# The second phase of an attention and gated-MLP kernel: seven block products for eight of its feed-forward blocks instead of four

## The chip, the cores and the metric

The kernel runs on one core of a Trainium2 chip, as one program. The metric is the device time of that program in microseconds (us). The engines named below are TensorE (PE; its weight loads are PEld), VectorE (DVE), ScalarE (ACT) and SyncE (SP, whose queue issues all the DMAs). SBUF is the memory on the core, PSUM holds what TensorE accumulates, in banks of 512 fp32 columns.

## The reference

```python
def phi(x):
    proj = np.einsum('bhsd,df->bhsf', x, w_phi)
    proj = proj - np.max(np.abs(proj), axis=-1, keepdims=True)
    return np.concatenate([np.exp(proj), np.exp(-proj)], axis=-1)
q_p, k_p = phi(q), phi(k)                       # 8 batches, 8 heads, 576 tokens, 64 -> 256
kv = np.einsum('bhsf,bhsd->bhfd', k_p, v)
num = np.einsum('bhsf,bhfd->bhsd', q_p, kv)
den = np.einsum('bhsf,bhf->bhs', q_p, np.sum(k_p, axis=2))[..., None] + 1e-06
x = (num / den).transpose(0, 2, 1, 3).reshape(4608, 512)
gate = 1.0 / (1.0 + np.exp(-(x @ w_gate)))      # 512 -> 1536
return (gate * (x @ w_val)) @ w_out             # 1536 -> 512
```

## The kernel before

The 4608 tokens of `x` go through the feed-forward part in twelve blocks `j` of 128 of its 1536 features. To keep near fp32 accuracy, each operand of a matmul is split into a high part of type fp32r and the remainder, and each product is three matmuls (high x high, high x low, low x high).

First phase: attention over 32 pairs of heads (`attend`), and, as soon as 512 tokens of `x` (a chunk, nine in all) are there, the blocks 0 to 3 on that chunk (`first_js`). `gate` computes one block's gate and value products, 12 matmuls of 512 columns each (L909), and `mm_out` the output product (L957). The partial sums of the four blocks go to DRAM (`yscr`), the chunks of `x` too (`xscr`). The gate is made of Tanh(g/2) and Exp(g) on ScalarE, and on VectorE of a mask (L933) and two multiplies with the value (L938, L943); the factor 2 that this leaves is taken out by the 0.5 in the output's scale (L980, L1109).

Second phase: blocks 4 to 7 in the same way on all nine chunks (`gate(NCH + C, j, ...)`), with the chunks of `x` fetched and split again (`load_x`, L884 to L893), the partial sums of the first phase added (`finish`, L1109) and written to DRAM again (`y2scr`). Then blocks 8 to 11 with seven block products instead of eight: the 768 x 512 block of `x` is cut into four quarters, from which `x_blocks` makes seven operands (fetches L1180, subtractions L1191, splits L1200 on ScalarE and L1204 on VectorE), `combine` makes seven operands of the weights of a pair of blocks (L1043, L1057, L1066, L1071), `group` does the seven products of 6 matmuls of 384 columns (L1247) and adds their results up on VectorE (L1260), `gated` and `valued` make `h` (L1285 to L1327), and the output product is L1354. A pass over 768 tokens has four groups (two pairs of blocks, gate and value) and 72 output matmuls; six such passes (`dc`) cover the tokens. The weights of each matrix come packed as 64-bit words and are unpacked by `weigh` (load L788, then L793 to L864 on VectorE, L797 and L826 on ScalarE).

Memory: `Area.ring` cuts four arenas into slots; slots of different stages overlap, and a slot is taken when its last user has ended. `low` and `flat` are there from the start, `high` and `more` take the place of the attention's tiles when these are done (`swap`).

Order: the code only lists operations with a rank, their inputs, outputs and slots. `Plan.run` puts them into one list per engine by a planner: of the operations that could start soonest, the one of lowest rank. Each engine runs its list in order, so an operation that waits holds all that stands behind it, DMA issues on SP's queue included.

Of the kernel before, what the change touches and what calls it, by code (L numbers as in the profile page):

```python
# [20 lines left out]
P = 128  # L21
NP = H // 2
DM = H * D
# [11 lines left out]
JB = 8  # L35
# [5 lines left out]
RB = 84 << 10  # L41
FB = 3 << 10
NQ4 = JB - JA
NQ = 3
ONPE = 12
# [13 lines left out]
HSTEP = 2.0  # L59

# [206 lines left out]
def attention_moe(  # L267
# [62 lines left out]
    wscr = [dram.tile([2, P, DM], F32, tag=f"wo{c}", name=f"wo{c}") for c in range(NJ - JB)]  # L330
# [7 lines left out]
    r_wh, r_wl = (x.ring(JA, 3 * DM) for _ in range(2))  # L338
    r_xh, r_xl = (x.ring(XN, CW) for _ in range(2))
    r_hh, r_hl = (x.ring(HN, CW) for _ in range(2))  # L340
# [4 lines left out]
    r_top = x.ring(2, DM, U32)  # L345
    x = high()
    r_w2 = x.ring(2 * NQ4, 3 * DM)
    r_wh2, r_wl2 = r_w2[::2], r_w2[1::2]
    r_zh, r_zl = x.ring(6, CW), x.ring(6, CW)
    r_k = x.ring(6, CW)  # L350
    x = low(56)
    r_zh2, r_zl2 = r_zh + x.ring(2, CW), r_zl + x.ring(2, CW)
    r_y1 = x.ring(4, DM)
    r_wst = x.ring(7, DM)
    r_G = low().ring(8, 7 * 2 * P)
    r_X = low(56).ring(10, 2 * HT)
    x = high()
    r_X += x.ring(4, 2 * HT)
    r_h = x.ring(8, 2 * HT)
    r_y1b = x.ring(4, DM)  # L360
    r_wo = high(48).ring(8, DM)
    r_f = flat().ring(5, HT)
    x = flat(12)
    r_tmp = x.ring(3, 2 * HT)
    r_f += x.ring(7, HT) + more().ring(FB // (4 * HT), HT)
# [18 lines left out]
    def on_act(n, fn, reads, writes, rank):  # L384
        return plan.op("ACT", 0.08 + n / 1200, 0.17, fn, reads, writes, rank)
# [17 lines left out]
    closing, opening, feeding = [], [], []  # L403
# [467 lines left out]
    def weigh_all(j, r, step, deep, rings):  # L871

        wh, wl = Buf([rings[0]], [P, 3 * DM]), Buf([rings[1]], [P, 3 * DM])
        weights[j] = [(wh, wl), []]
        for m in range(3):
            weigh(j, m, r + step * m, deep(m), wh, wl, slice(m * DM, m * DM + DM), m)
# [22 lines left out]
    def gate(c, j, r, banks, parted=False, rings=(r_hh, r_hl)):  # L899
# [3 lines left out]
        def product(o, m, c0, c1):  # L903
            (wh, wl), _ = weights[j]
# [20 lines left out]
        u, t = Buf([r_u], [P, CW]), Buf([r_t], [P, CW])  # L925
        hh, hl = Buf([rings[0]], [P, CW]), Buf([rings[1]], [P, CW])
        z = -100.0
        on_act(CW, lambda: act.activation(t(), g(), AF.Tanh, scale=0.5), [g], [t], z)  # L928
        on_act(CW, lambda: act.activation(u(), g(), AF.Exp), [g], [u], z)  # L929

        def positive():
# [14 lines left out]
        on_act(CW, lambda: act.copy(hh(), u()), [u], [hh], z)  # L946
        dve(
            CW, lambda: vec.tensor_tensor(hl(), u(), hh().bitcast(F32), op=ALU.subtract),  # L948
            [u, hh], [hl], z,
        )  # L950
        return hh, hl

    def mm_out(acc, t, hs, j, first, last):
        (hh, hl), (wh, wl) = hs, weights[j][0]
        ts, ws = slice(t * P, t * P + P), slice(2 * DM, 3 * DM)
        for i, (a, w) in enumerate(((hh, wh), (hh, wl), (hl, wh))):
            nc.tensor.matmul(  # L957
                acc(), a()[:, ts], w()[:, ws], start=first and i == 0, stop=last and i == 2
            )

    def first_js(c, r, step):
# [5 lines left out]
        for t in range(CW // P):  # L967
            acc, y = Buf(banks, [P, DM]), Buf([r_y], [P, DM])

            def go(t=t, acc=acc):  # L970
# [5 lines left out]
                [x for h in hs for x in h] + [(x, 2) for i in range(JA) for x in weights[i][0]],  # L976
# [3 lines left out]
                DM, lambda y=y, acc=acc: act.activation(y(), acc(), AF.Copy, scale=0.5),  # L980
# [7 lines left out]
    for i in range(N):  # L988
# [4 lines left out]
        if i < 4:  # L993
            weigh_all(
                i, WAT + 3 * WSTEP * i, WSTEP, lambda m, i=i: 3 * i + m >= RAW, (r_wh, r_wl)
            )
        if i % NP == NP - 1:
            lo = 0 if i < NP else ((i // NP) * S) // CW
            for c in range(lo, ((i // NP + 1) * S) // CW):
                r = due(i + 1) + LEAD + 66.0 * (c - lo)  # L1000
                if c:
                    fed = len(plan.ops)
                    load_x(c, r - 20.0, [(r_xh, r_xl)])
                    feeding += plan.ops[fed:]
# [15 lines left out]
    for j in range(JA, JB):  # L1020
        weigh_all(j, base + 10.0 * (j - JA), 3, lambda m: False, (r_wh2, r_wl2))

    blocks, wo, combined = {}, {}, []
    names = ["11", "12", "S3", "22", "S1", "S2", "S4"]
    KH = 2 * P

    def combine(n, m, r):

        gh, gl = Buf([r_G], [P, 7 * KH]), Buf([r_G], [P, 7 * KH])
        blocks[n, m] = gh, gl  # L1030
        w, x = Buf([r_mid], [P, 4 * KH], F32), Buf([r_mid], [P, 4 * KH], F32)

# [3 lines left out]
        for i in range(2):  # L1036
            weigh(
                JB + 2 * n + i, m, r + 3 * i, False, gh, gl,
                slice(2 * i * KH, 2 * (i + 1) * KH), i, [done],
# [7 lines left out]
                [(gh, i), (gl, i)], [(w, i)], r + 5, after=combined[-1:],  # L1047
            )
        for o, a, b, op, reads in (
            (0, (w, 2), (w, 3), ALU.add, [(w, 1)]),  # L1050
            (1, (x, 0), (w, 0), ALU.subtract, [(w, 0)]),
            (2, (w, 1), (x, 1), ALU.subtract, [(w, 0)]),
            (3, (w, 0), (w, 2), ALU.subtract, [w]),
# [4 lines left out]
                    of(x, o), of(*a), of(*b), op=op  # L1058
                ),
                reads, [x], r + 5.5 + o / 10,  # L1060
            )
        combined.append(plan.ops[-1])
        for n_, o, i in ((3, 4, 0), (1, 2, 3)):
            part = 2 if o == 4 else 1
            on_act(
                n_ * KH, lambda n_=n_, o=o, i=i: act.copy(of(gh, o, n_), of(x, i, n_)),  # L1066
# [365 lines left out]
```

## Time and profile before

| | |
|---|---|
| median of 3 runs (lowest to highest) | 1185.74 us (1184.75 to 1186.16) |
| the profiled execution | 1183.81 us |
| its span, first to last instruction | 1182.0 us |
| TensorE's clock | 1.0 throughout |
| end of attention's matmuls | 514 us |
| first matmul of the first seven-product pass | 901 us |
| last matmul | 1178.4 us |

The page gives the busy time of each engine over the span, the waits tell whom an engine waited for, the chain is the work that ended last followed back from the end, and windows give busy times for a stretch. In a timeline the first number is the start, the second the length of an instruction from start to end; instructions of one engine overlap a little at their ends, so that the distance between two starts is what an instruction costs in a row of them. Matmuls are pipelined: their lengths (337 to 395 ns) say nothing, the distance between their starts does.

### The profile page before, as it was taken

Reading aid. Unit: us, or ns where it says so; the run is one execution under the profiler, and the core shown is the slowest. Engines: PE = TensorE matmul, PEld = TensorE weight load, DVE = VectorE, ACT = ScalarE, POOL = GpSimd, SP = SyncE. Lnnn points to the kernel's source line nnn. Section 1 sums busy time; section 2 is a strip of 40 time slices with the busy share of each in tenths; the row PEclk is TensorE's granted clock in tenths of the full one; section 3 lists DMA queues with packets and bytes.
Section 4 is the critical chain, followed back from the end, with each engine's and each line's share of the span. In section 5 each row is a group of like instructions: output and inputs, shape, how many; then the busy total and the mean of one; then the engine's idle time right before and its main releaser. Section 6 shows DMA issues by size and latency. Waiting matters only on the chain.

```text
span 1182.0 us, 21892 instructions
## 1 busy us (share of the span) xinstructions
PE 1166.2 (99%) x8652; PEld 928.0 (79%) x8652; DVE 904.0 (76%) x1755; ACT 591.4 (50%) x1128; POOL 0.7 (0%) x6
## 2 busy tenths in 40 slices
PE   8999999999999999999999999999999999999998
PEld 6676666667766767778888888888888999999997
DVE  6999989888888788669836997444446978878885
ACT  6867776666666566545533453232223443433432
POOL 0000000000000000000000000000000000000000
PEclk9999999999999999999999999999999999999999
DMA  6764553533444342334416544223333235135132
GB/s 232 217 223 139 159 186 89 171 116 113 133 134 137 86 157 87 113 108 157 141 36 226 173 145 169 95 84 107 120 123 110 60 105 157 42 120 161 41 108 72
DMA packets 90223, 152.18 MB, mean 129 GB/s; under 512 B 18312, under 2 KB 33800, under 8 KB 90120
## 3 DMA queue, kind: packets, MB, share of 16 engines
q1 hardware_dynamic: 90120, 150.78, 40.3%
q8 instruction: 68, 1.11, 0.4%
q14 instruction: 35, 0.29, 0.1%
HBM read 110.62 MB, written 39.98 MB: 127 GB/s over the span
## 4 chain that ended last, share of the span: by engine, by line
PE 83%; DVE 8%; DMA 5%; ACT 2%; issue 1%; SPq 0%; DVEq 0%
PE gate L909 22%; PE bank L1247 14%; PE bank L957 9%; PE gate L1354 8%; PE bank L909 7%; PE gate L957 6%; PE bank L618 4%; PE bank L660 3%; DMA rb<-den 2%; PE bank L429 2%; PE bank L678 2%; DMA den<-dn 1%; PE bank L534 1%; DVE d L584 1%; PE bank L632 1%
## 5 line engine op out<-in xcount | busy, mean ns | idle before, releaser
L909 PE MATMUL gate<-low 128*128 128x512 f32 x744 | 177.0, 394 | 1.2 <-ACT flat L929 0.6
L909 PEld LDWEIGHTS gate<-low 128*128 128x128 f32 x744 | 137.7, 188 | 31.6 <-issue 1.2
L1247 PE MATMUL bank<-low 128*128 128x384 f32 x728 | 151.9, 337 | 0.4 <-DVE low L1204 0.4
L1247 PEld LDWEIGHTS bank<-low 128*128 128x128 f32 x728 | 129.0, 188 | 1.2 <-DVE low L1204 0.7
L909 PE MATMUL gate<-high 128*128 128x512 f32 x468 | 113.6, 390 | 0.0
L476 ACT ACTIVATE ek<-ek 128x512 f32<-128x512 f32 (+1 forms) x192 | 96.7, 526 | 27.9 <-DVE ek L464 26.6
L957 PE MATMUL bank<-high 128*128 128x512 f32 x432 | 105.1, 392 | 0.2 <-DVE high L948 0.2
L909 PEld LDWEIGHTS gate<-high 128*128 128x128 f32 x468 | 87.9, 188 | 18.7
L1354 PE MATMUL gate<-high 128*128 128x512 f32 x432 | 99.1, 390 | 0.0
L957 PEld LDWEIGHTS bank<-high 128*128 128x128 f32 x432 | 81.0, 188 | 18.2 <-DVE high L948 0.6
L1354 PEld LDWEIGHTS gate<-high 128*128 128x128 f32 x432 | 81.1, 188 | 16.5
L957 PE MATMUL gate<-low 128*128 128x512 f32 x384 | 92.8, 395 | 0.0
L938 DVE SCALAR_TENSOR_TENSOR flat<-flat,gate 128x512 f32<-128x512 f32 x66 | 45.2, 685 | 57.8 <-PE gate L909 57.2
L957 PEld LDWEIGHTS gate<-low 128*128 128x128 f32 x384 | 70.9, 188 | 15.4 <-issue 1.0
L618 PE MATMUL bank<-ek,vin 128*32 128x256 f32 x1240 | 73.3, 381 | 4.0 <-ACT d L542 3.2
L933 DVE TENSOR_SCALAR flat<-flat 128x512 uint32<-128x512 uint32 x72 | 30.2, 419 | 58.9 <-ACT flat L928 58.9
L618 PEld LDWEIGHTS bank<-ek,vin 128*32 128x32 f32 x1240 | 37.5, 110 | 45.1 <-issue 9.8
L1247 PE MATMUL bank<-high,low 128*128 128x384 f32 x280 | 72.3, 335 | 0.0
L1260 DVE TENSOR_TENSOR flat<-flat,bank 128x384 f32<-128x384 f32 x98 | 54.0, 551 | 20.2 <-PE bank L1247 19.5
L946 ACT CAST high<-flat 128x512 fp32r<-128x512 f32 x36 | 22.3, 621 | 90.6 <-DVE flat L943 90.6
L435 DVE TENSOR_REDUCE mk<-bank 128x4 f32<-128x512 f32 (+1 forms) x92 | 49.1, 553 | 19.8 <-PE bank L429 17.1
L943 DVE SCALAR_TENSOR_TENSOR flat<-flat 128x512 f32<-128x512 f32 x72 | 49.6, 689 | 4.0
(210 smaller groups left out, 2049.2 us busy)
## 6 DMA issues: line engine op xcount, KB each, us to landing
flat<-w_moe SPq DMA_DIRECT2D x36, 512.0 KB
low<-xs SPq DMA_DIRECT2D x49, 256.0 KB
kin<-k SPq DMA_DIRECT2D x32, 320.0 KB
qin<-q SPq DMA_DIRECT2D x32, 320.0 KB
vin<-v SPq DMA_DIRECT2D x32, 320.0 KB
ys<-flat SPq DMA_DIRECT2D x36, 256.0 KB
yt<-flat SPq DMA_DIRECT2D x36, 256.0 KB
high<-yt SPq DMA_DIRECT2D x36, 256.0 KB
```

Of the source, the lines that this page charges most:

```text
L435: vec.tensor_reduce(mx, pk, axis=AX.X, op=ALU.max, apply_absolute_value=True)
L476: lambda g=g, sg=sg: act.activation(ek[g]()[:, :, sg * F : sg * F + F], ek[g]()[:, :, F:], AF.Exp, scale=1.0 - 2.0 * sg,),
L618: nc.tensor.matmul(o_[o : o + Q, : 2 * F], vx()[:, 2 * t + hd, o % D : o % D + Q], (e0, e1)[hd][:, t, :] if t < 4 else e2[:, 0, :], start= ...
L660: nc.tensor.matmul(nm()[o : o + Q, :], w()[:, sg, o : o + Q], es[sg]()[:, o // D, cs], start=sg == 0, stop=sg == 1, tile_position=(0, o),)
L909: nc.tensor.matmul(o(), a()[:, ws], x(), start=cc + n == 0, stop=cc == NC4 - 1 and n == 2,)
L933: vec.tensor_scalar(tu, tu, 0x7FFFFFFF, None, op0=ALU.bitwise_and)
L938: lambda: vec.scalar_tensor_tensor(t(), t(), 1.0, vl(), op0=ALU.add, op1=ALU.mult),
L943: lambda: vec.scalar_tensor_tensor(u(), u(), 1.0, t(), op0=ALU.min, op1=ALU.mult),
L957: nc.tensor.matmul(acc(), a()[:, ts], w()[:, ws], start=first and i == 0, stop=last and i == 2)
L1247: nc.tensor.matmul(o()[:, :HT], s()[:, ws], y()[:, cc, :], start=first and cc + i_ == 0, stop=cc + i_ == 3, skip_group_check=not first,)
L1260: lambda: vec.tensor_tensor(o(), p(), q()[:, :HT], op=ALU.add),
L1354: nc.tensor.matmul(acc(), s()[:, h, o : o + P], w(), start=n + i + k_ == 0, stop=n == NB - 1 and i == 1 and k_ == 2,)
```

## The change

- Blocks 4 to 7 of the second phase are done like blocks 8 to 11. There are two passes of six times 768 tokens: one over the pairs of blocks (4,5) and (6,7), with the partial sums of the first phase going to `y2scr`, one over (8,9) and (10,11), which ends in `out`. The same slots serve both.
- The combined weights of the first pass are made at the end of the first phase, straight into the slots `r_G` and `r_wo` of the `high` arena. Those of the second pass are made during the first four 768-token steps of the first pass, one matrix pair and one output matrix a step, in two staging slots (`r_stage`), written to DRAM (`kept`, to `gscr` and `wscr`) and fetched into the first pass's slots as these come free (`fetched`). The blocks of `x` (`r_X`) now lie in `low` where the first phase's weights lie.
- From chunk 7 of the first phase on, the gate is ScalarE's Sigmoid and one multiply, with no factor 2; `exps` keeps these behind every earlier operation of ScalarE.

```diff
+    if c >= LATE:                                   # in gate(); LATE = 7
+        on_act(CW, lambda: act.activation(u(), g(), AF.Sigmoid), [g], [u], z, exps)
+        dve(CW, lambda: vec.tensor_tensor(u(), u(), vl(), op=ALU.mult), [vl], [u], z)
+    else:
+        halved(g, vl, u, z)
...
-    for C in range(NCH):
-        r0 = base + 200.0 + span * C
-        load_x(NCH + C, r0 - 20.0, [(r_zh2, r_zl2) if C > 1 else (r_zh, r_zl)], [last] + [fed] * (C > 1))
-        for i, j in enumerate(js):
-            hs = gate(NCH + C, j, r, [r_g, r_a], False, (r_k, r_k))
-            for t in range(4):
-                pe(
-                    "f", 0.685,
-                    lambda acc=acc, t=t, hs=hs, j=j, i=i: mm_out(
-                        acc, t, hs, j, i == 0, i == len(js) - 1
-                    ),
...
-    for dc in range(NDC):
-        r = base2 + 46.0 * dc
-        x = x_blocks(dc, r - 20.0)
+    def pass_over(ns, dc, r, ws, wo, src, mark, dst, dmark):
+        x = x_blocks(dc, r - XLEAD)
+        for i, n in enumerate(ns):
+            hs.append([(Buf([r_h], [P, 2, HT]), Buf([r_h], [P, 2, HT])) for _ in range(2)])
+            gs = gated(group(ws[n, 0], x, r + 14.6 * i))
+            valued(gs, group(ws[n, 1], x, r + 14.6 * i + 7.3), hs[i])
...
+    for n in range(2):
+        r = base - 30.0 + 30.0 * n
+        for m in range(2):
+            ws[n, m] = combine(n, m, r + 10.0 * m, [r_G], [])
+        for j in pair(n):
+            wo[j] = out_weight(j, r + 20.0, [r_wo], [])
+    start = base + 150.0
+    for dc in range(NDC):
+        r = start + SPAN * dc
+        pass_over((0, 1), dc, r, ws, wo, yscr, ymark, lambda c, t: y2scr[c][t], y2mark)
+        if dc < 4:
+            n, m = 2 + dc // 2, dc % 2
+            kept(combine(n, m, r + KEEP, [r_stage], [done]), gscr[n, m], mark, r + KEEP)
+            j = JA + 4 + dc
+            kept(out_weight(j, r + KEEP + 10.0, [r_stage], [done]), wscr[j], mark, r + KEEP)
+    start += SPAN * NDC
+    for n, m, late in ((2, 0, []), (2, 1, taken[-4:-3]), (3, 0, outs[-8:-7]), (3, 1, outs[-1:])):
+        ws[n, m] = fetched([r_G], 7 * KH, gscr[n, m], marks[n, m], start, late)
+    for j in (*pair(2), *pair(3)):
+        wo[j] = fetched([r_wo], DM, wscr[j], marks[j], start + 10.0)
+    for dc in range(NDC):
+        pass_over((2, 3), dc, start + SPAN * dc, ws, wo, y2scr, y2mark, final, None)
```

The changed kernel's lines stand elsewhere: L913 and L970 are the full gate and output products, L1228 and L1310 those of the seven-product form, L1241 its adds, L1279 and L1287 the multiply and the remainder of `h`, L1177 and L1190 the subtractions and splits of `x`, L795 to L866 the unpacking of weights, L1068 to L1093 their combination, L1138 the sum with the partial result, L1166 the fetches of `x`, L1133 those of partial sums, L1142 the results' stores, L1106 and L1117 the weights' way to DRAM and back.

How the order moves, at three places. First TensorE's list at the end of the first phase (`gate` and `bank` are PSUM banks, `low` and `high` the arenas of the operands). Before:

```order
L909 MATMUL bank4_192<-low_313 128x512 x12
L909 MATMUL gate1_201<-low_313 128x512 x12
L957 MATMUL bank0_168<-high_5431 128x512 x3
L957 MATMUL bank3_182<-high_5431 128x512 x3
L957 MATMUL bank2_180<-high_5431 128x512 x3
L957 MATMUL bank1_170<-high_5431 128x512 x3
L909 MATMUL gate0_194<-high_5431 128x512 x12
L957 MATMUL gate2_207<-low_313 128x512 x12
```

Now:

```order
L913 MATMUL bank3_194<-low_325 128x512 x12
L1228 MATMUL bank2_192<-low_325,high_5441 128x384 x6
L1228 MATMUL bank1_182<-low_325,high_5441 128x384 x6
L970 MATMUL gate1_213<-low_325 128x512 x12
L970 MATMUL gate0_206<-low_325 128x512 x12
L970 MATMUL gate2_219<-low_325 128x512 x12
L970 MATMUL bank0_180<-low_325 128x512 x12
L1228 MATMUL bank4_204<-low_325,high_5441 128x384 x6
```

The second phase's full products (operands in `high`), which were woven into the end of the first phase, are gone; two products of the first seven-product group come ahead of the last chunk's output products.

Second, VectorE's list in the last group of a seven-product step (`flat` and `more` hold sums on the way). Before, in the first step:

```order
L1296 TENSOR_SCALAR flat_163<-flat_163 128x384 x2
L1260 TENSOR_TENSOR flat_163<-flat_163,bank4_192 128x384
L1260 TENSOR_TENSOR more_7935<-flat_163,bank0_168 128x384
L1260 TENSOR_TENSOR more_7935<-more_7935,bank2_180 128x384
L1191 TENSOR_TENSOR flat_163<-flat_163,low_313 128x768
L1309 SCALAR_TENSOR_TENSOR more_7935<-more_7935,bank3_182 128x384
```

Now, in the second step of the first pass:

```order
L1241 TENSOR_TENSOR flat_175<-flat_175,bank0_180 128x384
L850 SCALAR_TENSOR_TENSOR flat_175<-flat_175 128x512
L1241 TENSOR_TENSOR more_5903<-flat_175,bank3_194 128x384
L858 TENSOR_SCALAR flat_175<-flat_175 128x512
L795 TENSOR_SCALAR flat_175<-flat_175 128x512
L1241 TENSOR_TENSOR more_5903<-more_5903,bank1_182 128x384
L1177 TENSOR_TENSOR flat_175<-more_5903,low_325 128x768
L1279 TENSOR_TENSOR flat_175<-flat_175,bank4_204 128x384
```

Steps of the weights' unpacking stand between the adds; the masks (L1296) are gone.

Third, SP's list in the last step of the first pass; before, each such step had only the quarters of `x`, partial sums and results there:

```order
L1166 DMA more_5903<-xs1_89 128x2x256
L1117 DMA high_5441<-g20_127 128x1792 x2
L1166 DMA low_325<-xs0_88 128x2x384
L1166 DMA low_325<-xs0_88 128x2x128
L1117 DMA high_5441<-g21_128 128x1792 x2
L1166 DMA low_325<-xs0_88 128x2x384
L1166 DMA low_325<-xs1_89 128x2x256
L1117 DMA high_5441<-g30_129 128x1792 x2
L1133 DMA low_325<-ys8_105 128x512
L1142 DMA yt7_113<-flat_175 128x512
```

The second pass's combined weights (`g20` to `g30`) are fetched between the quarters of its first block of `x`.

More of the change, by code (lines that the diff above doesn't have):

```diff
@@ L345, in attention_moe @@
     r_top = x.ring(2, DM, U32)
-    x = high()
[L347 to L361, printed above, removed]
+    x = low()
+    r_X = x.ring(14, 2 * HT)
+    r_y1 = x.ring(3, DM)
+    r_h = x.ring(8, 2 * HT)
+    r_stage = x.ring(2, 7 * 2 * P)
+    x = high()
+    r_G = x.ring(8, 7 * 2 * P)
+    r_wo = x.ring(8, DM)
+    r_x7 = high(42).ring(2 * NC4, CW)
+    r_sum = flat(20).ring(1, 2 * DM)
+    r_tmp = flat(24).ring(1, 2 * HT)
     r_f = flat().ring(5, HT)
-    x = flat(12)
-    r_tmp = x.ring(3, 2 * HT)
-    r_f += x.ring(7, HT) + more().ring(FB // (4 * HT), HT)
+    x = more()
+    r_tmp += x.ring(2, 2 * HT)
+    r_f += x.ring(6, HT)
     at_rings = {}
@@ L903, in product @@
         def product(o, m, c0, c1):
-            (wh, wl), _ = weights[j]
+            wh, wl = weights[j][0]
             for cc in range(c0, c1):
@@ L999, in attention_moe @@
             for c in range(lo, ((i // NP + 1) * S) // CW):
+                if c == LATE:
+                    exps.append(
+                        plan.op(
+                            "X", 0.0, 0.0, lambda: None,
+                            after=[o for o in plan.ops if o.eng == "ACT"],
+                        )
+                    )
                 r = due(i + 1) + LEAD + 66.0 * (c - lo)
@@ L1046, in combine @@
                 ),
-                [(gh, i), (gl, i)], [(w, i)], r + 5, after=combined[-1:],
+                [(gh, i), (gl, i)], [(w, i)], r + 5,
             )
[L1049 to L1053, printed above, removed]
+        for o, a, b, op in (
+            (3, 2, 3, ALU.add),
+            (2, 0, 2, ALU.subtract),
+            (0, 3, 0, ALU.subtract),
+            (1, 1, 0, ALU.subtract),
         ):
@@ L1108, in finish @@
             DM,
-            lambda: vec.scalar_tensor_tensor(
-                y(), acc(), 0.5, y1().bitcast(F32), op0=ALU.mult, op1=ALU.add
-            ),
+            lambda: vec.tensor_tensor(y(), acc(), y1().bitcast(F32), op=ALU.add),
             [acc, y1], [y], -90.0,
         )
-        sp(256 << 10, lambda: nc.sync.dma_start(dst(c, t), y()), [y], mark(c, t), r)
-        return got
-    js = list(range(JA, JB))
-    span = 33.0
-    y2mark = [Buf() for _ in range(NCH)]
-    loads = []
@@ L1148, in attention_moe @@
-    turn = plan.op("X", 0.0, 0.0, lambda: None, after=loads + staged)
-    base2 = base + 200.0 + span * NCH
-    for j in range(JB, NJ):
-        wo[j] = Buf([r_wo], [P, DM]), Buf([r_wo], [P, DM])
-        for n in range(2):
-            sp(
-                256 << 10,
-                lambda x=wo[j][n], j=j, n=n: nc.sync.dma_start(
-                    x().bitcast(F32), wscr[j - JB][n]
-                ),
-                [wmark[j, n]], [wo[j][n]], base2 - 10.0, [turn],
-            )
+        sp(
+            256 << 10, lambda: nc.sync.dma_start(dst(c, t), y()), [y],
+            [(dmark[c], t)] if dmark else [], r,
+        )
@@ L1227, in x_blocks, with group @@
         return at_
-    prior = [turn]
-    XB = ("11", "T2", "T3", "T1", "21", "T4", "22")
-    taken = [turn]
-    def group(n, m, x, r):
-        gh, gl = blocks[n, m]
+    def group(weight, x, r):
+        gh, gl = weight
         a, b, c, d = (Buf([r_a], [P, CW]) for _ in range(4))
```

272 lines of the change are left out of this document (127 added, 145 removed).

## The prediction

> **What bounds the kernel now.** I read the head of the page first, then the chain that ended last in order of time, TensorE's list of waits, busy time by stage, and last VectorE's instructions one by one. The page and the waits (us in total, times, longest):
>
> ```profile
> span 1182.0 us, 21892 instructions
> PE 1166.2 (99%) x8652; PEld 928.0 (79%) x8652; DVE 904.0 (76%) x1755; ACT 591.4 (50%) x1128; POOL 0.7 (0%) x6
> HBM read 110.62 MB, written 39.98 MB: 127 GB/s over the span
> PE bank L429 <- DMA kin<-k: 4.4, 1, 4.4
> PE bank L1247 <- DVE low L1204: 0.4, 1, 0.4
> PE bank L957 <- DVE high L948: 0.2, 1, 0.2
> ```
>
> TensorE is busy all the time, and in the second phase it waits for 0.4 and 0.2 us only. So the kernel is as long as its list of matmuls, and the question has two parts: how much shorter the list gets, and whether the others keep up with the new one. The chain gives start, length and count of each stretch:
>
> ```profile
> 514.41 16.54 PE gate L909 x72
> 703.74 5.44 PE gate L909 x24
> 736.38 5.52 PE gate L909 x24
> 933.92 16.33 PE gate L1354 x72
> 995.94 29.32 PE bank L1247 x168
> 1162.01 16.38 PE gate L1354 x72
> 1178.41 0.69 DVE flat L1109
> ```
>
> A 512-column matmul takes 5.44/24 = 0.2267 us, in every second chunk 5.52/24 = 0.2300; a 384-column one of the seven-product form takes 29.32/168 = 0.1745. The stages, and a stretch in which the DMA engines are loaded (busy us of PE, PEld, DVE, ACT and POOL with counts; then PE clock, DMA share, GB/s):
>
> ```profile
> 522.90:613.20 90.30, 68.68 (x127) 1.00 0.40 129
> 530.00:540.00 10.00, 10.00 (x46) 8.24 (x45) 9.19 (x19) 7.64 (x15) 0.00 (x0) 1.00 0.56 211
> 640.00:650.00 10.00, 10.00 (x45) 8.26 (x44) 9.81 (x20) 2.39 (x6) 0.00 (x0) 1.00 0.87 290
> 950.26:979.55 29.29, 29.29 (x169) 29.29 (x169) 21.49 (x46) 12.68 (x26) 0.00 (x0) 1.00 0.33 98
> 995.94:1041.59 45.65, 45.65 (x241) 42.84 (x241) 38.30 (x71) 18.50 (x35) 0.00 (x0) 1.00 0.34 103
> ```
>
> (The first of these rows is VectorE alone.) A seven-product pass over 768 tokens takes TensorE 45.65 us. VectorE is busy for 38.30 of them, the highest of the others, and idle for 7.35: it is the engine to watch.
>
> **TensorE's list.** Until 514.41 both lists are the same. From there to 933.92, 419.5 us, TensorE does what is left of the first phase, 34 units of 12 matmuls (ten of chunk 6, twelve each of chunks 7 and 8), 34 x 12 x 0.2267 = 92.5 us; the groups of one seven-product pass, 29.3; and the full products of blocks 4 to 7. These are left: 419.5 - 92.5 - 29.3 = 297.7 us for 108 units, 1296 matmuls, the two waits among it. The change takes them out and puts in six more passes of 168 + 72 matmuls, 6 x (29.32 + 16.33) = 273.9. **Net -23.8 us.** The profiled execution took 1183.81, its span 1182.0; with -23.8 and nothing else it would be 1160.0.
>
> The gain per column is thinner than 7/8, since a shorter matmul pays the same fixed part: 384 columns cost 0.1745/0.2267 = 77% of 512, not 75%. And PEld is busy for 29.29 of 29.29 us while the groups run. The Trainium skill (Perfetto Trace Analysis, Identifying the Most-Contended Engine) asks to judge TensorE's headroom by LDWEIGHTS busy time instead of matmul busy time; by that rule the groups are at the limit of the weight loads and shorter matmuls bring nothing more. The trace does not contradict it, but the 0.1745 was measured under these very loads, so the sum stands either way.
>
> Bounds. The products now read weights from the high arena and blocks from low; before, 728 of 1008 read low alone and the rest both, at one pace, so 0. The output products of all twelve passes take `h` from low and weights from high. L1354 has both in high (16.33 for 72). The other end is the chunk whose operands lie in both: 864 x (0.2300 - 0.2267) = 2.9 us. I take **+1.0**, nearer to L1354.
>
> **The handover.** VectorE's paces, from instructions that followed each other without a wait (start, us):
>
> ```profile
> 558.79 0.42 DVE L856 TENSOR_SCALAR flat<-flat 128x512 uint32<-128x512 uint32 x1
> 559.12 0.42 DVE L793 TENSOR_SCALAR flat<-flat 128x512 uint32<-128x512 uint32 x1
> 559.46 0.69 DVE L864 SCALAR_TENSOR_TENSOR high<-flat 128x512 fp32r<-128x512 uint32 x1
> 560.06 0.68 DVE L938 SCALAR_TENSOR_TENSOR flat<-flat,bank 128x512 f32<-128x512 f32 x1
> 546.00 0.69 DVE L820 SCALAR_TENSOR_TENSOR flat<-flat 128x512 uint32<-128x512 uint32 x1
> 546.72 0.43 DVE L840 TENSOR_SCALAR flat<-flat 128x512 uint32<-128x512 uint32 x1
> 963.79 0.55 DVE L1316 SCALAR_TENSOR_TENSOR flat<-flat 128x384 f32<-128x384 f32 x1
> 964.26 0.55 DVE L1260 TENSOR_TENSOR flat<-flat,bank 128x384 f32<-128x384 f32 x1
> 989.10 0.94 DVE L1204 TENSOR_TENSOR low<-flat,high 128x768 fp32r<-128x768 f32 x1
> 989.97 1.81 DVE L1204 TENSOR_TENSOR low<-flat,low 128x768 fp32r<-128x768 f32 x2
> L1057 DVE TENSOR_TENSOR flat<-flat 128x256 f32<-128x256 f32 x16 | 6.7, 421 | 0.0
> 522.90 0.69 DVE L864 SCALAR_TENSOR_TENSOR high<-flat 128x512 fp32r<-128x512 uint32 x1
> ```
>
> So 0.34 us for a mask of 512, 0.60 for a two-operand step of 512, 0.47 of 384, 0.87 of 768, and 0.42 less the overlap of 0.08 = 0.34 of 256; a step that reads its predecessor's result starts 0.72 after it instead of 0.60, some 0.13 more. Before, the first write to the new arena was at 522.90. In the new list VectorE has 146 instructions from there to the last part of the first blocks: 70 x 0.60 + 64 x 0.34 + 11 x 0.87 + 0.47 = 73.8 us. The last part is wanted by the seventh product, at 514.4 + 92.5 + 6 x 1.05 = 613.2, so 90.3 us are there and 16.5 are left for waits. The same stretch held 68.68 us of VectorE before without harm. One place is late by my count: chunk 8's last value product ends at 596.1, VectorE then owes two steps of 0.60 and T2's remainder of 0.87, and the second early product wants it at 597.1. **+1.3** for the handover. Ends: 0, and 8 if half of the 16.5 us turns out to be missing.
>
> ScalarE gains a table load in this stretch, because Sigmoid follows Exp and Tanh. The row of the one at the start:
>
> ```profile
> L476 ACT ACT_TABLE_LOAD x1 | 1.3, 1283 | 0.7 <-PEq L1382 0.7
> ```
>
> 1.3 us once, on an engine that is 50% busy and loses an Exp or a Tanh from each gate: 0. The Trainium skill (ScalarE: Activation LUTs, What ACT_TABLE_LOAD costs) adds a drain of 1.38 us to each switch; no run here shows it. By it the handover would be 2.7 us on ScalarE and, at worst, as much later.
>
> **The passes.** Each pass loses eight masks and eight multiplies on VectorE. What stays is 36 steps of 384, 11 of 768 and 6 of 512: 16.9 + 9.6 + 3.6 = 30.1 us of 45.65. The first four carry a weight preparation each: three matrices of 3 x 0.34 + 3 x 0.60 = 2.8, two sums of 512 and eight steps of 256, in all 8.5 + 1.2 + 2.7 = 12.4, so 42.5 us. That leaves 3.1 us of each 45.65, where 7.35 were idle. I laid the paces along the order of the second pass, from the start G of its last group to the next pass's start at G + 7.3 + 16.3 = G + 23.7: the five adds and the weight steps between them follow the banks; the eight value steps end at G + 11.4; the last block part ends at G + 21.6, and the product that wants it comes at G + 30; the next pass's first add is due at G + 26.0, and VectorE is free for it at G + 25.9. No product waits, but hardly any slack is left. **+1.0** for the four; 0 to 26, the rival below. The eight unloaded passes: 0.
>
> **The turn between the passes.** 8 x 0.92 MB of block weights and 8 x 0.26 MB of output weights are read back, 9.4 MB, while some 6.3 MB of x, partial sums and results also move, between the first free slot, 7 us into the last pass, and the first output products, 29 us into the next: 67.5 us. At the 290 GB/s above that is 54 us, at 211 it is 74. The block loads stand ahead of loads and stores on SP's queue, which then wait too, but for work due later. **+1.0**, from 0 to 7.
>
> Sum: 1160.0 + 1.0 + 1.3 + 1.0 + 1.0 = 1164.3. The median of the runs, 1185.74, lies 1.9 above the profiled execution; so **1166 us**.
>
> **Rivals.**
> *VectorE bounds the loaded passes (ends slower).* If the 7.35 us of idle time stay, because they are waits for transfers and for ScalarE that the order doesn't fill, and each of the 18 steps of the weight chains runs as a dependent one (+0.13, 2.3 us), a loaded pass takes 42.5 + 7.35 + 2.3 = 52.2, +6.5, and four cost 26: 1162.9 + 26 = 1189. It decides from 6 us a pass, 23.8/4. For it: 93% load. Against it: the weight steps stand between the adds, where VectorE now waits for TensorE. 5%. In between, with 2 to 5 us a pass, it is 1171 to 1183, about 1176: 15%.
> *The turn.* At 211 GB/s 7 us late: 1172. 7%.
> *The saving isn't there.* If weight loads, with their 188 ns each,
>
> ```profile
> L1247 PEld LDWEIGHTS bank<-low 128*128 128x128 f32 x728 | 129.0, 188 | 1.2 <-DVE low L1204 0.7
> ```
>
> set the pace of the new passes, each takes 168 x 0.188 + 16.33 = 47.9 and the list shrinks by 10.2 only: 1179. 29.32 for 168 speaks against it. 4%.
> *Little moves*, by several of these: 1%.
>
> **How the numbers follow.** The forecast has 68%. The range goes from 1160 (no stall, and no difference between profiled execution and median) to 1178, which takes in the turn and most of the half-bound passes. A measurement tells about 0.2% (2.4 us) from no change. Faster: 68 + 15 + 7 + 4 less the 1 of the in-between case that ends too near = 93%; same 1 + 1 = 2%; slower 5%.
>
> **What would show it.** Right: 2016 seven-product matmuls at 0.1745, twelve passes of some 45.7 us, VectorE over 41 us busy in the first four and near 32 later, TensorE's waits under 5 us beyond those at the start. Wrong: passes one to four longer than the rest, with waits of L1228 for VectorE or ScalarE; a gap at the first pass or at the turn; an unequal pace of L1228 or L1310.

## The result, and the profile after

The changed kernel takes 1167.3 us (median of 4 runs, 1165.75 to 1167.91), the kernel before 1185.95 beside it (4 runs, 1184.75 to 1186.37): a ratio of 0.9842, 95% interval 0.9825 to 0.9859. The profiled execution took 1167.91 us with a span of 1166.0. The forecast was 1166 with a range from 1160 to 1178.

The head of the page after, and TensorE's waits from 500 us to the end (us in total, times, longest):

```profile
span 1166.0 us, 22301 instructions
PE 1148.7 (99%) x8796; PEld 939.5 (81%) x8796; DVE 933.6 (80%) x1793; ACT 583.3 (50%) x1115; POOL 0.7 (0%) x6
HBM read 117.96 MB, written 47.32 MB: 142 GB/s over the span
```

```profile
PE bank L1228 <- DVE low L1190: 0.7, 1, 0.7
PE bank L1228 <- ACT low L1186: 0.2, 1, 0.2
```

The number of matmuls rises from 8652 to 8796, TensorE's busy time falls by 17.5 us: many matmuls of 512 columns have become more of 384. VectorE and the traffic grow, and TensorE waits for little: 0.9 us from 500 us to the end, at the first two seven-product groups. The chain, in order of time:

```profile
516.39 16.54 PE gate L913 x72
...
557.83 8.40 PE gate L913 x36
...
613.37 27.04 PE bank L1228 x156
640.41 16.79 PE gate L1310 x72
657.21 29.13 PE bank L1228 x168
...
870.01 13.99 PE gate L1310 x60
...
890.97 24.97 PE bank L1228 x144
```

Three things are to be seen. The steps follow each other without a gap: five steps of 29.13 + 16.79 after 640.41 end at 870.01, which is where the sixth's output products start, and the turn to the second pass (870 to 916) has no hole either. The output products are slower than L1354 before, 16.79 for 72 instead of 16.33; the product groups are a little faster, 29.13 for 168 instead of 29.24 to 29.32 in the five full stretches before. And the first row, up to which both kernels have the same list, starts 1.98 us later than its counterpart at 514.41.

VectorE's busy time in the six steps of the first pass:

```profile
613.40:659.20 45.80, 39.05 (x72) 1.00 0.46 148
659.20:705.10 45.90, 43.41 (x80) 1.00 0.60 193
705.10:751.00 45.90, 43.48 (x83) 1.00 0.62 205
751.00:797.00 46.00, 43.75 (x82) 1.00 0.54 176
797.00:843.00 46.00, 35.26 (x63) 1.00 0.47 151
843.00:889.00 46.00, 32.05 (x54) 1.00 0.55 192
```

Up to 43.75 of 46.00 us, and in this execution still nobody waits. The preparation does not keep to steps 1 to 4: VectorE is busy for 39.05 us only in the first, and the fifth still has four L1082 and four L1093 of it.

Where the 16.0 us between the two spans come from: TensorE's list -23.8; attention's end +2.0; from there to 640.41 it took 124.0 us where 92.5 + 29.3 = 121.8 were counted, +2.2; twelve output stretches 12 x 0.46 = +5.5; eleven product stretches 11 x -0.19 = -2.1 (by the 29.32 that the prediction took; by the mean of the five, 29.27, it is -1.6). Sum -16.2.

### The profile page after: what moved, and what is told of

Same layout as the page of the kernel before. It is cut to its first block, busy times and chain, and to the rows that moved or that the text cites. A ratio compares the mean times of both kernels' runs of the same rounds, so it can differ in the third digit from the quotient of the medians.

```text
span 1166.0 us, 22301 instructions
## 1 busy us (share of the span) xinstructions
PE 1148.7 (99%) x8796; PEld 939.5 (81%) x8796; DVE 933.6 (80%) x1793; ACT 583.3 (50%) x1115; POOL 0.7 (0%) x6
## 4 chain that ended last, share of the span: by engine, by line
PE 85%; DVE 8%; DMA 5%; ACT 1%; issue 1%; SPq 0%; DVEq 0%; ACTq 0%
PE bank L1228 30%; PE gate L1310 17%; PE gate L913 11%; PE gate L970 7%; PE bank L620 4%; PE bank L662 3%; PE bank L431 2%; DMA rb<-den 2%; PE bank L680 2%; PE bank L913 2%; PE bank L536 1%; DMA den<-dn 1%; PE bank L970 1%; DVE d L586 1%; PE bank L634 1%; PE bank L646 1%
## 5 line engine op out<-in xcount | busy, mean ns | idle before, releaser
L1228 PE MATMUL bank<-low,high 128*128 128x384 f32 x2016 | 352.3, 336 | 0.9 <-DVE low L1190 0.7
L1228 PEld LDWEIGHTS bank<-low,high 128*128 128x128 f32 x2016 | 349.8, 188 | 2.7 <-DVE low L1190 1.0
L1310 PE MATMUL gate<-high,low 128*128 128x512 f32 x864 | 203.6, 395 | 0.0
L1310 PEld LDWEIGHTS gate<-high,low 128*128 128x128 f32 x864 | 162.3, 188 | 37.9
L913 PE MATMUL gate<-low 128*128 128x512 f32 x708 | 168.4, 394 | 1.2 <-ACT flat L948 0.6
L913 PEld LDWEIGHTS gate<-low 128*128 128x128 f32 x708 | 130.8, 188 | 30.2 <-issue 1.2
L1241 DVE TENSOR_TENSOR more<-more,bank 128x384 f32<-128x384 f32 x104 | 57.2, 550 | 43.0 <-PE bank L1228 42.8
L970 PE MATMUL gate<-low 128*128 128x512 f32 x372 | 89.8, 395 | 0.0
L970 PEld LDWEIGHTS gate<-low 128*128 128x128 f32 x372 | 68.6, 188 | 15.0 <-issue 1.0
L1241 DVE TENSOR_TENSOR flat<-flat,bank 128x384 f32<-128x384 f32 x87 | 47.9, 551 | 34.9 <-PE bank L1228 34.2
L620 PEld LDWEIGHTS bank<-ek,vin 128*32 128x32 f32 x1240 | 37.4, 110 | 45.8 <-issue 10.2
L1138 DVE TENSOR_TENSOR flat<-gate,low 128x512 f32<-128x512 f32 x72 | 49.3, 685 | 24.8 <-PE gate L1310 15.0
L1186 ACT CAST low<-more 128x768 fp32r<-128x768 f32 x36 | 30.1, 836 | 66.2 <-DVE more L1177 66.2
L466 DVE TENSOR_TENSOR ek<-bank,mk 128x512 f32<-128x512 f32 (+1 forms) x92 | 48.2, 550 | 0.6 <-ACT d L549 0.2
L589 ACT ACTIVATE eq<-d 128x1152 f32<-128x1152 f32 x29 | 33.9, 1167 | 24.5 <-DVE d L586 24.4
L431 PE MATMUL bank<-wk,kin 64*128 64x128 f32 x496 | 38.5, 289 | 4.5 <-DMA kin<-k 4.4
```

The costliest lines, as they stand in the source:

```text
L431: nc.tensor.matmul(pk[hd]()[:, t, :], x()[head(hd), t * P : t * P + P], wk[head(hd), :], start=True, stop=True,)
L466: vec.tensor_tensor(ek[g]()[:, :, F:], src, mk[g]()[:, :ns].unsqueeze(2).broadcast_to([P, ns, F]), op=ALU.subtract,)
L620: nc.tensor.matmul(o_[o : o + Q, : 2 * F], vx()[:, 2 * t + hd, o % D : o % D + Q], (e0, e1)[hd][:, t, :] if t < 4 else e2[:, 0, :], start= ...
L913: nc.tensor.matmul(o(), a()[:, ws], x(), start=cc + n == 0, stop=cc == NC4 - 1 and n == 2,)
L970: nc.tensor.matmul(acc(), a()[:, ts], w(), start=first and i == 0, stop=last and i == 2)
L1138: lambda: vec.tensor_tensor(y(), acc(), y1().bitcast(F32), op=ALU.add),
```

## Experiments

Two questions were put to the chip. First, the theory behind the forecast (A): TensorE's list alone sets the time, and VectorE and the transfers are hidden. Its rivals are that part of the gain came from relieving VectorE, or that VectorE or the turn is a limit that just happens not to show. Second, where the 5.5 us in the output products come from: from operands that lie in two arenas, or from addresses, or from something in the output products themselves.

### The changed kernel again, and only addresses moved

*again* is the changed kernel unedited. *wo_first* swaps two areas inside the arena `high`:

```diff
-    r_G = x.ring(8, 7 * 2 * P)
     r_wo = x.ring(8, DM)
-    r_x7 = high(42).ring(2 * NC4, CW)
+    r_G = x.ring(8, 7 * 2 * P)
+    r_x7 = high(56).ring(2 * NC4, CW)
```

Expected of *again*: 

> The changed kernel once more, on the chip on which the kernels beside it run, to compare them with and to see what varies from one execution to the next. Both theories: about 1167 us, 0.984 of before. The stretch up to the end of attention ended 2.0 us later in the changed kernel's profile than in that of before (516.4 against 514.4 us), with the same list on TensorE. If that is chance, the stretch ends somewhere between 514 and 517 here and in the other kernels, without regard to their memory layout; if the change made it, it ends at 516.4 +- 0.3 here and in every kernel with this layout of the first phase.

Expected of *wo_first*: 

> Only addresses change: in the arena high the output weights lie first (0 to 16 KB) and the block weights behind them (16 to 72 KB), instead of the other way round. Every engine's list is the same, and each operand stays in its arena. Theory A (arenas): output stretches 16.8 us, product stretches 29.1 us, total within 0.2% of the changed kernel. Rival C (addresses within an arena set the pace): one of the two moves, 0.1 us or more per stretch of 72 or 168.

Measured: *again* 1169.19 us (4 runs, 1166.69 to 1170.73), 0.9863 of before [0.9841, 0.9884]; *wo_first* 1167.24 (4 runs, 1166.53 to 1168.43), 0.9846 [0.9825, 0.9868]. The chain of *wo_first*:

```profile
516.39 16.54 PE gate L913 x72
640.40 16.79 PE gate L1310 x72
657.20 29.13 PE bank L1228 x168
```

The paces are those of the changed kernel to the last digit, so these addresses within the arena are out. The end of attention is at 516.38 and 516.39 in these two, 1.97 later than before, as if the change made it. The kernels below contradict that: with the same list up to there it lies at 514.42, 514.69, 514.80, 515.64, 513.89, 514.92 and, with one part of the change alone, at 513.68. One of those (515.64) has this very layout, another (513.89) differs from it only in the second pass. So the stretch varies by some 2.7 us from program to program, and the 2.0 us don't follow from what the change does. What sets them stays open.

*again* shows one thing that the first profile did not: its third step takes 47.05 us (703.12 to 750.17) instead of 45.92, with a wait of the output products for VectorE's sum,

```profile
PE gate L1310 <- DVE flat L1138: 0.5, 1, 0.5
```

and the chain goes back from there over VectorE's list and ScalarE's split of `x` (L1186) to a fetch of `x` that took 7.1 us. In *late_fetch* below the same step takes 46.88, in *wo_first* 46.25. So the loaded steps are close to their limit and not free in every execution of this list.

### The second pass's output weights into low, where h lies (wo_low_pass2)

```diff
-    r_y1 = x.ring(3, DM)
+    r_y1 = x.ring(2, DM)
...
     r_stage = x.ring(2, 7 * 2 * P)
+    r_wo2 = low(70).ring(8, DM)
...
-        wo[j] = fetched([r_wo], DM, wscr[j], marks[j], start + 10.0)
+        wo[j] = fetched([r_wo2], DM, wscr[j], marks[j], start + 10.0, stores)
```

(`stores` are the writes of the prepared weights; a third slot for partial sums comes from `high` in the second pass.) Expected: 

> The output weights of the second pass go to the arena low, where h lies; those of the first pass stay in high. Theory A (a 512-column matmul is slower when its two operands lie in different arenas): the 72 output matmuls of a step take 16.8 us in the first pass as before (0.233 each) and 16.33 in the second (0.2267 each), so 6 x 0.46 = 2.8 us less in all. Rival B (it is something of the output products themselves, such as the order of their weight loads or the result's banks): 16.8 in both passes and no change. Rival C (it is the address of the weights within their arena): any other pace in the second pass, unlike 0.2267.

Measured: 1163.78 us (4 runs, 1163.0 to 1165.42), 0.9821 of before [0.9801, 0.984]. Two neighbouring rows of each pass from the chain:

```profile
822.22 16.79 PE gate L1312 x72
839.01 29.13 PE bank L1230 x168
...
914.06 16.36 PE gate L1312 x72
930.41 29.12 PE bank L1230 x168
```

The first pass is its own control: 16.79 with `h` in low and weights in high, 16.36 with both in low, in one execution. Theory A, 0.43 us a step instead of the 0.46 foreseen.

### h into high as well, and two block weights into low (both_high)

In the second pass only, `h` goes to `high`, where its weights lie; the block weights of (10,11) go to `low`, where `x` lies. The first matrix of (10,11) is fetched a little later, with the second.

```diff
+    r_Ga, r_h2 = high().ring(4, 7 * 2 * P), high(28).ring(8, 2 * HT)
+    r_Gb = low(48).ring(4, 7 * 2 * P)
...
-            hs.append([(Buf([r_h], [P, 2, HT]), Buf([r_h], [P, 2, HT])) for _ in range(2)])
+            rh = r_h if dmark else r_h2
+            hs.append([(Buf([rh], [P, 2, HT]), Buf([rh], [P, 2, HT])) for _ in range(2)])
...
-    for n, m, late in ((2, 0, []), (2, 1, taken[-4:-3]), (3, 0, outs[-8:-7]), (3, 1, outs[-1:])):
-        ws[n, m] = fetched([r_G], 7 * KH, gscr[n, m], marks[n, m], start, late)
+    for n, m, late in ((2, 0, []), (2, 1, taken[-4:-3]), (3, 0, outs[-1:]), (3, 1, outs[-1:])):
+        ws[n, m] = fetched([r_Ga if n == 2 else r_Gb], 7 * KH, gscr[n, m], marks[n, m], start, late)
```

Expected: 

> Second pass only: h goes to high, where its output weights lie; the block weights of the pair (8,9) stay in high, those of (10,11) go to low, where the blocks of x lie. First pass as in the changed kernel. Theory A, in full (a 512-column matmul is slower with its operands in two arenas, a 384-column one faster, and which arena it is does not matter): output stretches 16.8 in the first pass and 16.36 in the second; products of (8,9) at 0.1734 us a matmul as everywhere in the changed kernel, those of (10,11) at 0.175, as the kernel before has them; so 29.25 for 168 instead of 29.12, and about 2 us less in all. Rival C (an address, or the arena low itself, is what helped): output stretches 16.8 in both passes. Rival J (the 384-column difference has to do with the kernel before's slots and not with arenas): 0.1734 for both pairs.

Measured: 1165.46 us (4 runs, 1162.85 to 1167.56), 0.9831 of before [0.9808, 0.9854]. The chain at the end of the first pass and in the second:

```profile
821.60 16.79 PE gate L1313 x72
838.39 29.13 PE bank L1230 x168
...
913.46 16.33 PE gate L1313 x72
929.79 29.15 PE bank L1230 x168
```

With both operands in high it is 16.33: neither arena is the fast one, it is the crossing that costs. The second half of theory A fell: a product step in which half of the matmuls have both operands in low takes 29.15, not the 29.25 expected, so 384-column matmuls don't care (0.1736 us from start to start for (10,11), 0.1734 for (8,9); means over the second pass). Rival J is right there. The traces say where the kernel before, with up to 29.32 for the same 168, loses its time: within a row of one kind the distances are 173 to 174 ns in both kernels, but before, products that read low alone and products that read both arenas take turns, 728 and 280 of 1008, and where they do, single distances reach 186 ns. In the changed kernel all 2016 are of one kind. No run tests this by itself.

### All output weights beside h (wo_low)

The first step keeps its own output weights in `high`, since `low` is still in use when they are made; they are written to DRAM too and fetched into `low` for the steps after it. The preparation for the second pass moves one step later, because its staging slots take the place of the first step's output weights.

```diff
-    r_y1 = x.ring(3, DM)
+    r_y1 = x.ring(2, DM)
     r_h = x.ring(8, 2 * HT)
-    r_stage = x.ring(2, 7 * 2 * P)
+    r_wo = x.ring(8, DM)
...
-    r_wo = x.ring(8, DM)
+    r_wo1 = x.ring(8, DM)
+    r_stage = high(56).ring(2, 7 * 2 * P)
+    r_y1 += high(70).ring(1, DM)
...
-            wo[j] = out_weight(j, r + 20.0, [r_wo], [])
+            wo0[j] = out_weight(j, r + 20.0, [r_wo1], [])
+            mark = marks[j] = Buf()
+            kept(wo0[j], wscr[j], mark, r + 30.0)
+            wo[j] = fetched([r_wo], DM, wscr[j], mark, base + 160.0, [done])
...
-        if dc < 4:
+        if 1 <= dc < 5:
```

Expected: 

> The output weights of all steps but the first of the first pass lie in low beside h; the first step keeps its own in high, from where they are also written to DRAM and fetched into low. The second pass's weights are prepared one step later, in steps 2 to 5. Theory A (two arenas slow a 512-column matmul): eleven of twelve output stretches take 16.33 instead of 16.8, 11 x 0.46 = 5.1 us less than the changed kernel, about 1162 us, if the handover and the loaded steps stay without a stall. Rival B (something of the output products themselves): no change, 1167, or slower by the 4.2 MB that move in addition. Rival D (VectorE or the queue has no room for the shifted preparation): waits of L1228 in steps 2 to 5, a us or more each.

Measured: 1162.08 us (1160.47 to 1163.05, 4 runs), 0.9803 of before [0.9784, 0.9823], where the changed kernel had 0.9863 [0.9841, 0.9884] on the same chip; the intervals don't meet. The chain, and all of TensorE's waits after 500 us:

```profile
637.24 16.86 PE gate L1312 x72
...
683.72 16.36 PE gate L1312 x72
700.07 29.12 PE bank L1230 x168
```

```profile
PE bank L1230 <- DVE more L1243: 0.2, 1, 0.2
```

Eleven of twelve stretches are at 16.36, 11 x 0.43 = 4.7 us less. The span is 1158.6, 7.4 below the changed kernel's: 4.7 of it in the output products, 1.7 at attention's end (514.69), which varies from program to program as said, and 1.5 on the way from there to the first output products (122.55 instead of 124.02 us). (The second step's products give 0.5 back: 29.62 us instead of 29.13.) Of that, 0.2 show as the wait above; no other wait of TensorE shows for the extra traffic and the shifted preparation, and the two at the handover are gone.

### Without Sigmoid (no_sigmoid)

The changed kernel with the gate's old form in chunks 7 and 8 and in both passes (Exp, Tanh, mask L1279, two multiplies; the output scaled by 0.5 in L1138):

```diff
-                HT, lambda t=t, src=src: act.activation(t(), src()[:, :HT], AF.Sigmoid),
-                [src] * (i == 0), [t], -100.0, exps,
+                HT, lambda u=u, src=src: act.activation(u(), src()[:, :HT], AF.Exp),
+                [src], [u], -100.0,
...
+                lambda t=t, src=src: act.activation(t(), src()[:, :HT], AF.Tanh, scale=0.5),
+                [src] * (i == 0), [t], -100.0,
...
+            dve(HT, positive, [], [t], -90.0, k=2.0)
...
-                lambda t=t, vl=vl: vec.tensor_tensor(t(), t(), vl()[:, :HT], op=ALU.mult),
+                    t(), t(), 1.0, vl()[:, :HT], op0=ALU.add, op1=ALU.mult
...
+                    u(), u(), 1.0, t(), op0=ALU.min, op1=ALU.mult
```

Expected: 

> The changed kernel with the gates as before: Exp, Tanh, the mask and two multiplies in chunks 7 and 8 and in both passes, the factor 2 taken out by the output's scale. VectorE, busy for 43.5 of the 46.0 us of a loaded step in the changed kernel, gets 8 masks of about 0.27 and 8 multiplies of 0.47 us more per step, 5.9 us: 49.4 us of work for 46.0. Theory A (VectorE's work is hidden as long as it fits, and fits by 2.5 us): steps 1 to 4 take about 3.4 us more each, with waits of the products for VectorE, 14 us in all, up to 20 with the handover; about 1181 to 1187 us, most of the gain gone. Rival E (the planner's order leaves work that can be put off, so that the excess is made up in steps 5 and 6): 0 to 5 us. Rival F (VectorE is the limit already): the whole 5.9 in each step, 24 us and more, 1191 or over.

Measured: 1171.57 us (4 runs, 1170.73 to 1172.28), 0.9891 of before [0.9864, 0.9919]; 4 us more than the changed kernel, not 14. (ScalarE gets an activation more for each gate, too.) VectorE in the six steps of the first pass:

```profile
613.40:659.20 45.80, 42.88 (x83) 1.00 0.46 144
659.20:705.10 45.90, 45.87 (x94) 1.00 0.57 196
705.10:751.00 45.90, 44.85 (x90) 1.00 0.49 169
751.00:797.00 46.00, 45.83 (x94) 1.00 0.51 154
797.00:843.00 46.00, 43.69 (x87) 1.00 0.47 153
843.00:889.00 46.00, 41.93 (x79) 1.00 0.68 249
```

In two steps VectorE is busy for 45.8 to 45.9 of 46 us, in the fifth for 43.69, where the changed kernel has 35.26. Of these 8.4 us, 7.0 are the masks (L1279) and second multiplies (L1299) themselves; the rest is about what one operation of the preparation (L822) takes, of which the fifth step of the changed kernel has none:

```profile
797.00:843.00 46.00, 1.38 (x2) 1.00 0.47 153
```

Three L1082 and four L1093 even lie in the sixth step. The preparation has slid into the fifth and sixth. Steps 1 to 4 keep their length (655.49 + 3 x 45.92 = 793.25, exactly where the fifth step's products start), and the loss comes only when the blocks of `x` for later steps are made too late: TensorE waits for L1192, and from 793.25 to the end of the pass's output products it takes 4.7 us more than the changed kernel (100.7 instead of 96.0).

```profile
PE bank L1230 <- DVE low L1192: 2.8, 3, 1.5
```

So theory A's size fell, and rival E holds: it isn't a step that has to hold its work, it is the pass. But the pass loses something before it is full (265 us of VectorE's work in these six rows, of 275.6), since the blocks of `x` fall due within it.

### The preparation twice (double_prep)

```diff
             n, m = 2 + dc // 2, dc % 2
+            combine(n, m, r + KEEP, [r_stage], [done])
+            out_weight(JA + 4 + dc, r + KEEP + 10.0, [r_stage], [done])
```

Expected: 

> Steps 1 to 4 of the first pass prepare each weight twice; the first copy is thrown away. That is 12.4 us more work for VectorE in each of four steps, 286.6 us where six steps have 276. Theory per step (what a step is given has to be done in it): steps 1 to 4 take some 9.9 us more each, 40 us, and the turn stays as it is. Theory of the pool (preparation has no due time before the turn; it is put off behind the products and fills the whole pass): no wait to speak of in steps 1 to 4, the steps 5 and 6 and the turn together late by the 11 us that six steps lack and by what the last weights need on their way through DRAM, 15 to 40 us, all after 850 us.

Measured: 1197.08 us in one run, 1.009 of before's median on that chip (1185.9); span 1195.3, 29.3 above the changed kernel. The chain around the turn, and the largest of TensorE's waits:

```profile
839.42 29.13 PE bank L1228 x168
...
882.54 1.05 PE bank L1228 x6
...
926.30 1.35 DVE low L1093 x4
927.67 5.11 DMA g<-low
932.84 5.43 DMA high<-g
```

```profile
PE bank L1228 <- DMA high<-g: 15.7, 2, 14.4
```

It is a single run, so without an interval. Up to 882 us nothing of TensorE's is late, with 55.9 us of VectorE's work handed to each of steps 1 to 4 of 45.9. Then all of it is: the last weights are made at 927 (L1093), go to DRAM in 5.1 us and come back in 5.4. A part of the loss is TensorE's clock: it was granted at 0.50 from 928 to 942 us, during the wait and behind it, and the first 22 products behind the wait took 6.60 us, where 22 x 0.1734 are 3.81. Here is the slower kernel of which the prediction's rival spoke; but it breaks at the turn, not in the loaded steps, and at twice the preparation.

### Sigmoid alone (sigmoid_alone)

The kernel before with Sigmoid and one multiply from chunk 7 on and in all of the second phase, full products of blocks 4 to 7 kept (the edit is the `LATE` part of the change's diff, and the same in `gated`). Expected: 

> The kernel before with one part of the change: Sigmoid and one multiply from chunk 7 on and in all of the second phase, full products of blocks 4 to 7 as before. Theory A (TensorE's list sets the time, and the gain of 24 us is the shorter list): the list is the same, TensorE waited for 0.6 us in all in that phase; 0 to -1 us, 0.998 to 1.001 of before. Rival G (part of the gain came from relieving VectorE): 5 us or more faster. Rival H (the table load and the order that it forces on ScalarE cost something): 2 us or more slower, with a wait of TensorE for ScalarE near 530 us.

Measured: 1184.12 us (10 runs, 1182.44 to 1186.21), 0.9989 of before [0.9976, 1.0002]. No change that can be told. TensorE's only wait after 500 us is this:

```profile
PE bank L1264 <- DVE low L1221: 0.2, 1, 0.2
```

So Sigmoid by itself brings nothing where VectorE had room, and 4 us in the changed kernel, where a loaded step leaves VectorE some 2.5 us.

### The block weights fetched late (late_fetch)

```diff
-    for n, m, late in ((2, 0, []), (2, 1, taken[-4:-3]), (3, 0, outs[-8:-7]), (3, 1, outs[-1:])):
+    for n, m, late in ((2, 0, outs[-1:]), (2, 1, outs[-1:]), (3, 0, outs[-1:]), (3, 1, outs[-1:])):
```

Expected: 

> The changed kernel, but the second pass's block weights are fetched only when the last output product of the first pass has been issued, all four matrices; before, the first one came as soon as its slots were free, some 30 us earlier. Theory A (the transfers at the turn are hidden because slots come free early): the first group waits for 1.84 MB, 6.3 us at 290 GB/s or 8.7 at 211 and some 2 us until the first data, the later groups for what their transfer takes beyond the 7.3 us of a group: 8 to 15 us in all, 1175 to 1182, all of it between 870 and 920 us. Rival I (the queue has room enough at any time): under 3 us.

Measured: 1180.02 us (10 runs, 1176.92 to 1183.76), 0.9953 of before [0.9935, 0.997]; span 1177.4, 11.4 above the changed kernel. The chain and the waits:

```profile
870.33 15.41 PE gate L1310 x66
887.93 8.71 DMA high<-g
896.69 30.63 PE bank L1228 x166
```

```profile
PE bank L1228 <- DMA high<-g: 8.6, 2, 7.4
```

The cover that the early slots give is worth 11 us: from 870 us to the next output products it takes 56.99 us here and 45.92 in the changed kernel. 8.6 of the 11.1 are waits. Another 1.8 are the pace behind them, 30.63 us for 166 products instead of 28.8 at 0.1734. TensorE had stood idle since 887.1, and its granted clock was 0.50 from 890 to 900 us; there its products start 320 ns apart, at full clock 173. One of these microseconds (after the clock's 0.50 stand the DMA share and GB/s):

```profile
897.00:898.00 1.00, 1.00 (x4) 1.00 (x4) 0.00 (x0) 0.00 (x0) 0.00 (x0) 0.50 1.03 423
```

In the changed kernel the eight fetches of `g` are issued from 848.2 us on (durations of the issue in ns, first and last start), here from 887.3 on. With the early issue TensorE waits for none of them; theory A's 8 to 15 us hold:

```profile
L1117 SPq DMA_DIRECT2D high<-g x8: 319/430/676, 848.2 to 892.6; - x8
```

## Why the prediction was right

**TensorE's list, -23.8.** Right. Its replacement, twelve passes of 168 + 72 matmuls, runs without gaps, and the part of the change that isn't the list (*sigmoid_alone*) gives 0.9989 [0.9976, 1.0002]. The part of the rule that judges headroom by LDWEIGHTS busy time (the Trainium skill, Perfetto Trace Analysis, Identifying the Most-Contended Engine) would see none in the new groups: 2016 loads are busy for 349.8 us, all of 12 x 29.13. The rival that priced a product at the 188 ns of its load is out: a step takes 45.92 us, not 47.9, since the loads overlap (2016 x 0.188 are 379 us).

```profile
L1228 PEld LDWEIGHTS bank<-low,high 128*128 128x128 f32 x2016 | 349.8, 188 | 2.7 <-DVE low L1190 1.0
```

**Products at an unchanged pace, 0.** 0.1734 instead of 0.1745 a matmul, -2.1 us. The row with 29.32 was the slowest of the five in the kernel before. "At one pace" does not hold for single matmuls: it is not the arena of a matmul that counts (*both_high*), but the kernel before loses some ns where the two kinds take turns. That reading is from the traces alone.

**Output products, +1.0, bounds 0 to 2.9.** This is the term that was mis-sized: +5.5, outside its bounds. The direction was seen, and the row that has it was quoted (5.52 for 24, operands in both arenas). The bound was half of what it should have been: in that row only 12 of the 24 matmuls have operands in both arenas (every second chunk of `x` had half of its slots in low), and 0.2300 is the mean of 0.2267 and 0.2333. Rows in which every matmul crosses have 0.2333: 8.40 for 36 with the weights in low and `x` in high, 16.79 for 72 here. The step that failed is "nearer to L1354": L1354 had both operands in one arena, and the change puts them in two, so it was the wrong neighbour. Moving the weights gives it back (*wo_low_pass2*, *wo_low*). One thing does not fit a price per matmul: in those chunks L957, with both operands in high, took 2.77 us for 12 instead of 2.72, and the single distances came back to 0.2267 only ten matmuls after the last crossing one. Why is open.

**Handover, +1.3.** Two waits, both at the first groups, for the splits of `x` (L1190, L1186) as foreseen: 0.9 us of idle time, and 1.5 us by the distances of starts (572, 1145 and 288 ns where 173 is the pace). Another 0.6 are 96 matmuls of chunk 7, which read `x` from high (0.2333 instead of 0.2267); that is the same term as above, and the prediction had not counted it here. That leaves 0.1 of the +2.2. The table load took its 1.28 us at 552.38, and the next instruction of ScalarE started at 553.68:

```profile
551.79 0.58 ACT L993 ACTIVATE flat<-gate 128x512 f32<-128x512 f32 x1
552.38 1.28 ACT L933 ACT_TABLE_LOAD   x1
553.68 1.09 ACT L933 ACTIVATE flat<-bank 128x512 f32<-128x512 f32 x2
```

There is no drain of 1.38 us beside it (the Trainium skill, ScalarE: Activation LUTs, What ACT_TABLE_LOAD costs, has one): the three rows follow each other within 0.02 us. In *sigmoid_alone* the load ends at 549.97 and the next instruction starts at 549.98.

**Loaded passes, +1.0.** 0 in the profiled execution, 1.1 in *again*. The count of 42.5 us was good to 1.3 in steps 2 to 4 (43.41 to 43.75 measured); the first step had 39.05, where over 41 was to be seen. But the condition under which it would matter was wrong. The rival let a step of 45.65 us hold all that is listed in it. *no_sigmoid* and *double_prep* show that the preparation gives way: the planner puts it behind whatever the products need, and it is due only at the turn. VectorE's limit is near the six steps of the pass, 276 us, against 237 us of work; 265 us cost 4.7, and 286.6 (as counted) cost 29. It doesn't decide from 6 us a step. (The rival's 1189 also starts too low: 1162.9 is 1160.0 + 1.0 + 1.9, without the handover and the turn; with them, as in the forecast, it would be 1191.)

**Turn, +1.0.** 0; the early fetches cover it, and 11 us are lost without them, 1.8 of these by TensorE's lower clock (*late_fetch*).

**Attention.** The prediction let it stand at 514.41. It was 516.39, and between 513.7 and 516.4 in eleven executions of kernels with the same list there. That is 2.0 of the result of which no step of the prediction spoke.

So the mechanism was right, and that the sum came out this near was in part luck, because terms of opposite error met: 1164.3 was foreseen for the profiled execution and 1167.91 measured, with +4.5 in the output products, +2.0 in attention, +0.9 in the handover, against -2.1 in the products and -2.0 for the two terms that were 0. The 1.9 us added from the profiled execution to the median were not there either: the median is 0.6 below it.

## What to carry to other kernels

Where one engine is busy 99% of the span, count its instructions by kind at their measured distance in the new form, and treat each other engine as a question of due times: work that is due only later slides, so a stage has to be judged by all of its steps together. It can lose a little before it is full, where something falls due within it (here 4.7 us at 265 of 276). Price a matmul by rows with its operands in the same places, not by its shape alone, and don't take a bound from a row that mixes two cases. When a placement costs 3% of a stretch, moving one buffer beside the other operand brought 0.4% of this kernel for a few lines.

## What the runs showed of the hardware

- A 512-column fp32r matmul that loads new weights each time takes 0.2267 to 0.2272 us with stationary and moving operand in the same of two SBUF areas (16.33 for 72 with both in the one, 16.36 with both in the other), 0.2333 with one in each (16.79 for 72). Other addresses within one area changed nothing (*wo_first*). For 384 columns there is no such difference (0.1734 and 0.1736), but some ns are lost where both kinds take turns (29.24 to 29.32 for 168 in the kernel before, 29.13 in the changed one).
- In *late_fetch* TensorE stood idle from 887.1 us on, and its granted clock was 0.50 from 890 to 900, the last 3 us of them with products one behind the other; these took 320 ns from start to start instead of 173. In *double_prep* the same was seen behind a longer wait.
- Exp, Tanh and Sigmoid: one table load of 1.28 us at the change from the first two to the third, and nothing else that shows.
- The same list of attention work ended at any time from 513.7 to 516.4 us from program to program, at 516.38 to 516.39 in three that differ in nothing that it uses and at 515.64 in a fourth. Why is open.
